# Two gated layers behind a block-sparse attention: token tiles of 512 columns in place of 384, x and the sums in one buffer each

## The chip, the cores and the metric

One core of a Trainium2 chip runs the kernel. The metric is device time in microseconds, the median of several runs. The engines are named as in the profile: PE (TensorE, matmuls), PEld (its weight loads), DVE (VectorE), ACT (ScalarE), POOL (GpSimd), SP (the engine whose queue issues most DMAs).

## What is computed

1536 tokens (2 batches of 768) pass through three stages in float32. The attention has 8 heads of 64; each query sees its neighbours within 16 positions and, for each block of 32 keys, one key (the block's maximum) with one value (the block's mean). Its outputs, one row of 512 numbers per token, feed two layers:

```python
a = softmax(concat(masked(scale * q @ k.T), scale * q @ k_max.T + log(32)))
x = (a @ concat(v, v_mean)).reshape(1536, 512)          # 8 heads side by side
x = (silu(x @ w_gate) * (x @ w_val)) @ w_out            # 512 -> 1536 -> 512
h = x @ w_in                                            # 512 -> 2048
out = (h * clip(h + 3, 0, 6) / 6) @ w_out2              # 2048 -> 512
```

## The kernel before

The layers' matmuls run on operands split in two parts (high and low, type float32r): `three` (L342) issues three matmuls for one product, high by high, low by high, high by low (L352 to L354). Their sum gathers in one PSUM bank of 128 partitions by up to 512 columns.

Tokens are the columns. They come in four tiles of T = 384 (L24, L25). The first layer's hidden units are done in N1 = 4 groups of G1 = 3 blocks of 128, the second's in N2 = 4 groups of G2 = 4 (L31 to L33). For each group and each tile `hidden1` (L437) makes two products per block (gate and value, 4 x 3 matmuls each), ACT takes the tanh out of the bank into u, DVE multiplies twice, and `split` (L420) makes the two parts of the result in a buffer g or gb: one ACT copy, one DVE or POOL subtraction. `out1` (L464) multiplies them by the output weights (4 x 3 x 3 matmuls) and ACT (first group) or DVE (the others) adds the bank into the sums `acc`. After the last group the sums are split again into x2, the second layer's input (L493 to L502). So a group of the first layer costs 72 + 36 = 108 matmuls per tile. `hidden2` (L505, 48 matmuls per group and tile) and `out2` (L525) do the same for the second layer, but out2 has the tokens on the partitions: blocks of 128 tokens, 512 columns of output weights as moving operand, 36 matmuls per tile. The very last block is done in two halves of 256 columns (L526), each stored by its own DMA.

Buffers before the change: one tile x0 to x3 per token tile of shape [128, 2 parts, 4, 384], used again for x2 (tags `x{t}`); one tile acc0 to acc3 of 1536 columns, used for v before and for the output sums afterwards (tags `acc{t}`); and, while attention has not reached them yet, the room of x3 holds three of the first keys (`early_k`, L567) and that of x2 the first queries (`early_q`, L568).

Weights arrive as raw words; `weights` (L378) turns each [128, 512] block into its two parts with five DVE passes (L389, L395, L399, L407, L299) and two ACT passes (L403, L292) (the last subtraction may go to POOL). Two sets of nine buffers, wa and wb, alternate from group to group.

The order is made by a planner (`Plan`, L101): every task has a rank, the engines it may use with an assumed duration, and the names that it reads and writes; `schedule` (L171) simulates the engines with the ring sizes of L280 (mm and mmb: banks, u: 3, g: 5, gb: 5) and issues each engine's instructions in the order it finds. Ranks are then replaced by latest start times and the plan is made anew, up to six times; the one with the earliest end is used (L247). The loop at L829 goes over (layer, group, tile); the hidden tasks of one tile are ranked together with the out tasks of the tile before (`prev`). The rings gb, wb and mmb exist only from the end of attention on (`swap`, L847). While group 0 of the first layer runs, attention for the next token tile is made beside it: its scores, exponentials and outputs go through the banks `at` and `pv` and end in x (L736 to L746).

Of the kernel before, what the change touches and what calls it, by code (L numbers as in the profile page):

```python
# [25 lines left out]
NB = T // QB  # L26
TR = NB // 2
# [250 lines left out]
def tile_kernel(ctx: ExitStack, tc: tile.TileContext, q, k, v, vu, w_gate, w_val, w_out1, w_in2, w_out2, cst, out):  # L278
    nc = tc.nc
    rings = dict(mm=4, mmb=4, at=3, pv=1, wa=9, wb=9, raw=3, bits=2, u=3, g=5, gb=5,  # L280
# [51 lines left out]
    ident = cs[:, :P]  # L332

# [86 lines left out]
    def split(rank, gn, u):  # L420

        add(rank, {"act": 0.43}, lambda: copy("act", new(gn, [P, 2, T], F32R)[:, 0, :], tiles[u]), r=[u], w=[gn])
        add(rank, {"pool": 1.3, "dve": 0.5},
            lambda e: less(e, tiles[gn][:, 1, :], tiles[u], tiles[gn][:, 0, :].bitcast(F32)), r=[u], w=[gn], port=True)
# [9 lines left out]
    xt, x2t, acc, oacc = {}, {}, {}, {}  # L434


    def hidden1(rank, g, t, f, late):  # L437
        bg, bv, u, gn = bank(late), bank(late), ("u", 0, g, t, f), g_name(0, g, t, f, late)

        def tanh():  # L440
            nc.scalar.activation(new(u, [P, T]), tiles[bg][:, :T], AF.Tanh, scale=0.5)

        def gate():
            nc.vector.scalar_tensor_tensor(tiles[u], tiles[u], 1.0, tiles[bg][:, :T], ALU.add, ALU.mult)

        def val():
            nc.vector.tensor_tensor(tiles[u], tiles[u], tiles[bv][:, :T], ALU.mult)  # L447

        for i, bk in enumerate((bg, bv)):
            rank = three(  # L450
                rank, bk, T,
                lambda c, i=i: parts(w_name(0, g, i, f), c * P, P),
                lambda c: (xt[t][:, 0, c, :], xt[t][:, 1, c, :]),
                KC,
                lambda c, i=i: [w_name(0, g, i, f), ("x", t, c)],
                early=g == 0 and t == 0,
            )
            if i == 0:
                add(rank, {"act": 0.4}, tanh, r=[bg], w=[u])
                add(rank, {"dve": 0.47}, gate, r=[bg], w=[u])  # L460
        add(rank, {"dve": 0.47}, val, r=[bv], w=[u])
        split(rank, gn, u)

    def out1(rank, g, t, d, late):  # L464
        bk = bank(late)
        three(
            rank, bk, T,
            lambda f: parts(w_name(0, g, 2, f), d * P, P),
            lambda f: parts(gn_of[0, g, t, f], 0, T),
            G1,  # L470
            lambda f: [w_name(0, g, 2, f), gn_of[0, g, t, f]],
        )
        rank += 1.5
        room = [("A", t)] if g == 0 else []

        def first():
            if t not in acc:
                a = xpool.tile([P, KC * T], F32, tag=f"acc{t}", name=f"acc{t}")
                acc[t] = a.rearrange("p (c t) -> p c t", c=KC)
            nc.scalar.activation(acc[t][:, d, :], tiles[bk][:, :T], AF.Copy, scale=0.5)  # L480

        def more():
            a = acc[t][:, d, :]
            nc.vector.scalar_tensor_tensor(a, tiles[bk][:, :T], 0.5, a, ALU.mult, ALU.add)

        if g == 0:
            add(rank, {"act": 0.4}, first, r=[bk], w=[("acc", t, d)] + room)
        else:
            add(rank, {"dve": 0.47}, more, r=[bk], w=[("acc", t, d)])
        if g < N1 - 1:  # L490
            return

        def high():  # L493
            if t not in x2t:
                x2t[t] = xpool.tile([P, 2, KC, T], F32R, tag=f"x{t}", name=f"x2_{t}")
            copy("act", x2t[t][:, 0, d, :], acc[t][:, d, :])

        def rest(e):
            less(e, x2t[t][:, 1, d, :], acc[t][:, d, :], x2t[t][:, 0, d, :].bitcast(F32))

        add(rank, {"act": 0.43}, high, r=[("acc", t, d)], w=[("x2", t, d)] + [("x", t, c) for c in range(KC)])
        add(rank, {"pool": 1.3, "dve": 0.47}, rest, r=[("acc", t, d)], w=[("x2", t, d)], port=True)  # L502


    def hidden2(rank, g, t, f, late):  # L505
        bk, u, gn = bank(late), ("u", 1, g, t, f), g_name(1, g, t, f, late)
        rank = three(
            rank, bk, T,
            lambda c: parts(w_name(1, g, 0, f), c * P, P),
            lambda c: (x2t[t][:, 0, c, :], x2t[t][:, 1, c, :]),  # L510
            KC,
            lambda c: [w_name(1, g, 0, f), ("x2", t, c)],
        )

        def relu():
            nc.scalar.activation(new(u, [P, T]), tiles[bk][:, :T], AF.Relu, bias=3.0)

        def clip():
            nc.vector.scalar_tensor_tensor(tiles[u], tiles[u], 6.0, tiles[bk][:, :T], ALU.min, ALU.mult)  # L519

        add(rank, {"act": 0.4}, relu, r=[bk], w=[u])
        add(rank, {"dve": 0.47}, clip, r=[bk], w=[u])
        split(rank, gn, u)

    def out2(rank, g, t, m, late, d0=0, n=DM):  # L525
        if (g, t, m, n) == (N2 - 1, NT - 1, T // P - 1, DM):  # L526
            out2(rank, g, t, m, late, 0, DM // 2)
            out2(rank + 1.4, g, t, m, late, DM // 2, DM // 2)
            return
        bk = bank(late)  # L530
        three(
            rank, bk, n,
            lambda f: parts(gn_of[1, g, t, f], m * P, P),
# [4 lines left out]
        rank += 2.6  # L538

        def first():  # L540
            if t not in oacc:
                a = xpool.tile([P, KC * T], F32, tag=f"acc{t}", name=f"oacc{t}")
                oacc[t] = a.rearrange("p (m d) -> p m d", d=DM)
            nc.scalar.activation(oacc[t][:, m, :], tiles[bk], AF.Copy, scale=1.0 / 6.0)

        def more():
            a = oacc[t][:, m, d0 : d0 + n]
            nc.vector.scalar_tensor_tensor(a, tiles[bk][:, :n], 1.0 / 6.0, a, ALU.mult, ALU.add)

        def store():  # L550
            r0 = t * T + m * P
            nc.sync.dma_start(out=out[r0 : r0 + P, d0 : d0 + n], in_=oacc[t][:, m, d0 : d0 + n])

        if g == 0:
            add(rank, {"act": 0.5}, first, r=[bk], w=[("o", t, m)] + [("acc", t, d) for d in range(KC)])
        else:
            add(rank, {"dve": 0.6}, more, r=[bk], w=[("o", t, m)])
        if g == N2 - 1:
            add(rank, {"dma": 0.73 * n / DM}, store, r=[("o", t, m)])
# [65 lines left out]
    def queries(rank, t, c):  # L625
# [94 lines left out]
    def outputs(rank, t, c):  # L720
# [105 lines left out]
    span_g, span_o1 = 2 * G1 * KC * 0.52, KC * G1 * 0.52  # L826
    span_h, span_o2 = G2 * KC * 0.52, T // P * G2 * 0.69
    seq = [(0, g, t) for g in range(N1) for t in range(NT)] + [(1, g, t) for g in range(N2) for t in range(NT)]
    for layer, g, t in seq + [(2, 0, 0)]:  # L829
        late = swap is not None  # L830
        if layer == 0:
            heads_ = [lambda r, f=f: hidden1(r, g, t, f, late) for f in range(G1)]
            span = span_g + (span_o1 if prev else 0)
        elif layer == 1:
            heads_ = [lambda r, f=f: hidden2(r, g, t, f, late) for f in range(G2)]
            span = span_h + (span_o1 if g == 0 and t == 0 else span_o2)
        else:
            heads_, span = [], span_o2
        if (layer, g) == (0, 0) and t + 1 < NT:
            span += SPAN  # L840
        tails = [lambda r, a=a: a[0](r, *a[1:], late) for a in prev]
        step(rank, span, heads_, tails)
        if (layer, g) == (0, 0):
            if t + 1 < NT:
                attention(rank + NEXT, t + 1, (span - NEXT_END) / NP)
            if t + 2 == NT:
# [45 lines left out]
```

## Time and profile before

| | us |
|---|---|
| runs, median of 3 (lowest to highest) | 641.5 (640.62 to 641.62) |
| profiled execution: span, first to last instruction | 638.7 |
| PE busy | 627.4 (98%) in 4492 matmuls |
| DVE busy | 433.9 (68%) |
| ACT busy | 278.8 (44%) |
| POOL busy | 46.4 (7%) |
| DMA | 54.07 MB |

The profile gives no time of the profiled execution beside its span. Matmuls are pipelined: the duration of one is longer than the distance to the next, so rates are read from the starts.

### The profile page before, as it was taken

The numbers are of one execution on the slowest core, as the hardware profiler recorded it, in microseconds if no ns is written. First come the engines' busy times: TensorE is split into PE (matmuls) and PEld (weight loads), VectorE is DVE, ScalarE is ACT, GpSimd is POOL, SyncE is SP. The second block draws the span as 40 slices with busy tenths as digits, with TensorE's granted clock in tenths as the row PEclk, the third lists the DMA queues.
The fourth block names the chain that finished last, engine by engine and source line by source line (L and its number), as shares of the span: only waits on it lengthen the run. The fifth ranks groups of instructions, "written<-read, shape, count | busy, mean of one in ns | idle before, by whom it ended". The sixth has DMA issues, their size and how long they took to land.

```text
span 638.7 us, 11402 instructions
## 1 busy us (share of the span) xinstructions
PE 627.4 (98%) x4492; PEld 589.8 (92%) x4492; DVE 433.9 (68%) x961; ACT 278.8 (44%) x647; POOL 46.4 (7%) x51
## 2 busy tenths in 40 slices
PE   7899999999999999999999999999999999999997
PEld 6787889999999999999999999999999999999996
DVE  5999954899997974397656995286639744344442
ACT  4896886456444431153323554355324422222220
POOL 1234422000000000000000000000000000000000
PEclk9999999999999999999999999999999999999999
DMA  8887340233331411023100323031301000000112
GB/s 314 267 265 233 86 153 3 100 134 131 131 134 65 139 60 67 0 71 129 67 0 1 103 97 100 1 109 56 100 0 67 0 1 1 0 2 1 49 50 99
DMA packets 18917, 54.07 MB, mean 85 GB/s; under 512 B 2608, under 2 KB 5168, under 8 KB 18864
## 3 DMA queue, kind: packets, MB, share of 16 engines
q1 hardware_dynamic: 18576, 52.74, 24.7%
q8 instruction: 35, 0.57, 0.4%
q10 hardware_dynamic: 288, 0.61, 0.3%
q14 instruction: 18, 0.15, 0.1%
HBM read 50.19 MB, written 3.15 MB: 84 GB/s over the span
## 4 chain that ended last, share of the span: by engine, by line
PE 90%; DVE 5%; DMA 2%; ACT 1%; issue 1%; POOL 0%; SPq 0%; POOLq 0%
PE mm L352 16%; PE mm L353 15%; PE mm L354 15%; PE mmb L352 14%; PE mmb L354 13%; PE mmb L353 13%; PE at_s L657 2%; PE pv L728 1%; DMA raw<-in_moe_w_gate 1%; DVE p L677 1%; PE at_t L714 1%; DMA vn<-in_v 1%; DVE ksum L599 1%; DVE v L612 0%; DVE wa L299 0%
## 5 line engine op out<-in xcount | busy, mean ns | idle before, releaser
L352 PE MATMUL mm<-x,wa 128*128 128x384 f32 x196 | 68.4, 349 | 0.0
L353 PE MATMUL mm<-x,wa 128*128 128x384 f32 x196 | 65.9, 336 | 1.1 <-DVE wa L299 1.0
L354 PE MATMUL mm<-x,wa 128*128 128x384 f32 x196 | 65.7, 335 | 0.0
L403 ACT ACTIVATE raw<-raw 128x512 f32<-128x512 f32 x68 | 46.1, 680 | 26.1 <-DVE bits L395 23.0
L353 PE MATMUL mmb<-x,wb 128*128 128x384 f32 x160 | 53.5, 335 | 0.0
L353 PE MATMUL mm<-x,wb 128*128 128x384 f32 x160 | 53.5, 335 | 0.0
L354 PE MATMUL mmb<-x,wb 128*128 128x384 f32 x160 | 53.5, 334 | 0.0
L354 PE MATMUL mm<-x,wb 128*128 128x384 f32 x160 | 53.5, 334 | 0.0
L352 PE MATMUL mm<-x,wb 128*128 128x384 f32 x160 | 53.5, 334 | 0.0
L352 PE MATMUL mmb<-x,wb 128*128 128x384 f32 x160 | 53.5, 334 | 0.0
L292 ACT ACTIVATE g<-u 128x384 fp32r<-128x384 f32 x61 | 32.0, 524 | 39.0 <-DVE u L519 20.5
L399 DVE SCALAR_TENSOR_TENSOR bits<-raw,bits 128x512 uint32<-128x512 uint32 x68 | 47.7, 702 | 0.1
L407 DVE SCALAR_TENSOR_TENSOR bits<-raw,bits 128x512 f32<-128x512 f32 x68 | 47.2, 696 | 0.6 <-ACT raw L403 0.2
L395 DVE SCALAR_TENSOR_TENSOR bits<-raw,bits 128x512 uint32<-128x512 uint32 x68 | 46.4, 684 | 0.3
L299 DVE TENSOR_TENSOR g<-u,g 128x384 fp32r<-128x384 f32 x57 | 31.9, 560 | 20.2 <-ACT g L292 20.1
L292 ACT ACTIVATE gb<-u 128x384 fp32r<-128x384 f32 x51 | 26.8, 525 | 37.5 <-DVE u L447 18.7
L353 PE MATMUL mmb<-x,wa 128*128 128x384 f32 x124 | 41.5, 335 | 0.0
L354 PE MATMUL mmb<-x,wa 128*128 128x384 f32 x124 | 41.5, 334 | 0.0
L352 PE MATMUL mmb<-x,wa 128*128 128x384 f32 x124 | 41.5, 334 | 0.0
L292 ACT ACTIVATE wb<-bits 128x512 fp32r<-128x512 f32 x32 | 20.2, 632 | 46.8 <-DVE bits L407 18.9
L299 DVE TENSOR_TENSOR gb<-u,gb 128x384 fp32r<-128x384 f32 x51 | 28.3, 556 | 17.2 <-ACT gb L292 17.2
L684 ACT ACTIVATE p<-p,st 128x120 f32<-128x120 f32 x96 | 36.7, 384 | 4.9 <-DVE st L677 4.9
(180 smaller groups left out, 1607.8 us busy)
## 6 DMA issues: line engine op xcount, KB each, us to landing
raw<-in_moe_w_out SPq DMA_DIRECT2D x28, 512.0 KB, 3.5
raw<-in_moe_w_in SPq DMA_DIRECT2D x16, 512.0 KB, 3.5
raw<-in_moe_w_gate SPq DMA_DIRECT2D x12, 512.0 KB, 3.7
raw<-in_moe_w_val SPq DMA_DIRECT2D x12, 512.0 KB, 3.5
vn<-in_v SPq DMA_DIRECT2D x8, 384.0 KB, 6.3
vw<-in_vu SPq DMA_DIRECT2D x16, 192.0 KB, 4.3
out<-oacc SPq DMA_DIRECT2D x11, 256.0 KB, 2.0
kT<-in_k SPq DMA_DIRECT2D x5, 400.0 KB, 7.7
```

What stands on the lines that cost most here:

```text
L292: nc.scalar.activation(dst, src, AF.Copy, scale=scale)
L299: eng[e].tensor_tensor(dst, a, b, ALU.subtract)
L352: nc.tensor.matmul(ps, lhsT=lh, rhs=rh, start=j == 0, stop=False)
L353: nc.tensor.matmul(ps, lhsT=ll, rhs=rh, start=False, stop=False)
L354: nc.tensor.matmul(ps, lhsT=lh, rhs=rl, start=False, stop=j == n_k - 1)
L395: nc.vector.scalar_tensor_tensor(t, high_w(), 0xC0000000, t, ALU.bitwise_and, ALU.bitwise_or)
L399: nc.vector.scalar_tensor_tensor(t, low_w(), 29, t, ALU.logical_shift_right, ALU.bitwise_or)
L403: nc.scalar.activation(mag, mag, AF.Abs)
L407: nc.vector.scalar_tensor_tensor(as_f(), mag, 2.0**-15, as_f(), ALU.is_ge, ALU.mult)
L599: nc.vector.tensor_reduce(ksum[c], kT[b, c][:, HALO : HALO + S].rearrange("q (n i) -> q n i", i=BLOCK), AX.X, ALU.max)
L657: nc.tensor.matmul(tiles["at", "s", *names[h]][a * QB : (a + 1) * QB, j, cols], lhsT=tiles[qt][hs, u * QB : (u + 1) * QB], rhs=rhs, start= ...
L684: nc.scalar.activation(a, a, AF.Exp, bias=s[:, 0, n : n + 1], scale=-1.0, accum_out=s[:, 1, n : n + 1])
```

## The change

The layers but for group 0 of the first take token tiles of 4 blocks of 128 (512 columns, 3 tiles); group 0, which runs beside attention, keeps tiles of 3 blocks (384 columns, 4 tiles). A tile is named by (first block, number of blocks). x and x2 share one buffer xs, and v, the first queries, acc and the output sums share one buffer accs; both are laid out by blocks of 128 tokens, so that a tile of either width is a slice. A tile's x for one part and one chunk of 128 features is 3 or 4 runs of 128 columns, 1024 elements apart. The dependencies that the planner is told are by block. The keys get buffers of their own; the first queries lie in accs behind v. u and g tiles grow to 512 columns, and the g ring shrinks from 5 to 4. The planner's assumed durations and spans follow the tile's width. The instructions of each tile, their engines and the weights' work stay as they were. Core of the diff (hidden2, the split, and the other copies follow the same pattern):

```diff
+TB = T // P
+BLOCKS = B * S // P
+WIDE = 4
...
-    rings = dict(mm=4, mmb=4, at=3, pv=1, wa=9, wb=9, raw=3, bits=2, u=3, g=5, gb=5,
+    rings = dict(mm=4, mmb=4, at=3, pv=1, wa=9, wb=9, raw=3, bits=2, u=3, g=4, gb=5,
...
+    xs = xpool.tile([P, BLOCKS, 2, KC, P], F32R, name="x")
+    accs = xpool.tile([P, BLOCKS, KC, P], F32, name="acc")
+
+    def xpart(lh, b0, nb, c):
+        return xs[:, b0 : b0 + nb, lh, c, :]
...
+    def tiles_of(layer, g):
+        nb = TB if (layer, g) == (0, 0) else WIDE
+        return [(b0, nb) for b0 in range(0, BLOCKS, nb)]
...
     def hidden1(rank, g, t, f, late):
+        (b0, nb), n = t, t[1] * P
...
-                rank, bk, T,
+                rank, bk, n,
                 lambda c, i=i: parts(w_name(0, g, i, f), c * P, P),
-                lambda c: (xt[t][:, 0, c, :], xt[t][:, 1, c, :]),
+                lambda c: (xpart(0, b0, nb, c), xpart(1, b0, nb, c)),
                 KC,
-                lambda c, i=i: [w_name(0, g, i, f), ("x", t, c)],
-                early=g == 0 and t == 0,
+                lambda c, i=i: [w_name(0, g, i, f)] + [("x", b, c) for b in range(b0, b0 + nb)],
+                early=g == 0 and b0 == 0,
...
-    early_k = xpool.tile([P, NP - 1, S + 2 * HALO], F32, tag="x3", name="early_k")
-    early_q = xpool.tile([P, 2, NP, T], F32, tag="x2", name="early_q")
-    kT = {(b, c): ap_.tile([P, S + 2 * HALO], F32, name=f"kT{b}_{c}") if b or c == NP - 1 else early_k[:, c]
-          for b in range(B) for c in range(NP)}
+    kT = {(b, c): ap_.tile([P, S + 2 * HALO], F32, name=f"kT{b}_{c}") for b in range(B) for c in range(NP)}
+
+    def acc_room(r, lo, n):
+        return accs[:, r * TB : (r + 1) * TB].rearrange("p b c t -> p (b c t)")[:, lo : lo + n]
...
-                tiles[n] = early_q[:, t, c]
+                tiles[n] = acc_room(q_room(t, c), S + c % 2 * T, T)
...
-    seq = [(0, g, t) for g in range(N1) for t in range(NT)] + [(1, g, t) for g in range(N2) for t in range(NT)]
+    seq = [(layer, g, t) for layer, groups in ((0, N1), (1, N2)) for g in range(groups) for t in tiles_of(layer, g)]
...
-                next_weights(*nxt, rank + span, 3 * span - W_END)
+                next_weights(*nxt, rank + span, len(tiles_of(layer, g)) * span - span - W_END)
```

## Rows read from the trace of the kernel before

**Rows 1.** The page: busy time of each engine, and PE in 40 slices.
```profile
PE 627.4 (98%) x4492; PEld 589.8 (92%) x4492; DVE 433.9 (68%) x961; ACT 278.8 (44%) x647; POOL 46.4 (7%) x51
...
PE   7899999999999999999999999999999999999997
...
PEclk9999999999999999999999999999999999999999
```

**Rows 2.** Engines by stretch (from:to us, length, busy us with instructions, clock).
```profile
core 0: us, PE busy (x) PEld busy (x) DVE busy (x) ACT busy (x) POOL busy (x), PEclk, DMA share, GB/s
0.00:26.23 26.23, 20.99 (x416) 17.99 (x416) 18.83 (x73) 16.31 (x59) 5.90 (x11) 1.00 0.87 286
26.23:50.00 23.77, 22.30 (x368) 18.62 (x368) 23.07 (x88) 21.45 (x76) 7.98 (x10) 1.00 0.86 278
50.00:70.00 20.00, 18.90 (x230) 16.77 (x230) 19.96 (x52) 13.64 (x42) 8.51 (x8) 1.00 0.61 188
70.00:109.00 39.00, 39.00 (x633) 34.35 (x632) 22.84 (x110) 30.05 (x108) 12.99 (x15) 1.00 0.26 83
109.00:136.35 27.35, 27.35 (x160) 27.35 (x158) 24.43 (x47) 13.45 (x25) 0.00 (x0) 1.00 0.27 97
136.35:360.99 224.64, 224.64 (x1298) 224.64 (x1297) 173.31 (x326) 86.72 (x156) 2.58 (x2) 1.00 0.24 80
360.99:634.93 273.94, 273.94 (x1401) 250.04 (x1401) 150.74 (x270) 97.21 (x184) 8.44 (x6) 1.00 0.13 42
```

**Rows 3.** Timeline of PE: first hidden matmuls of group 1 and of layer 2.
```profile
136.35 0.33 PE L352 MATMUL mmb<-x,wb 128*128 128x384 f32 x1
...
360.99 0.33 PE L352 MATMUL mmb<-x,wa 128*128 128x384 f32 x1
```

**Rows 4.** Timeline of PE: first and thirty-first matmul of a run of 512 columns.
```profile
620.56 0.39 PE L352 MATMUL mmb<-wb,gb 128*128 128x512 f32 x1
...
627.36 0.39 PE L352 MATMUL mmb<-wb,gb 128*128 128x512 f32 x1
```

**Rows 5.** Timeline of PE: the same place in two steps of layer 2, thirteen apart.
```profile
395.29 0.34 PE L352 MATMUL mm<-x,wa 128*128 128x384 f32 x1
...
611.69 0.34 PE L352 MATMUL mmb<-x,wb 128*128 128x384 f32 x1
```

**Rows 6.** Instruction groups by form: count, busy us, mean ns, idle before.
```profile
L395 DVE SCALAR_TENSOR_TENSOR bits<-raw,bits 128x512 uint32<-128x512 uint32 x68 | 46.4, 684 | 0.3
L389 DVE TENSOR_SCALAR bits<-raw 128x512 uint32<-128x512 uint32 x68 | 29.2, 432 | 0.1
L447 DVE TENSOR_TENSOR u<-u,mm 128x384 f32<-128x384 f32 x48 | 26.5, 551 | 13.1 <-PE mm L354 12.9
L299 DVE TENSOR_TENSOR wb<-bits,wb 128x512 fp32r<-128x512 f32 x29 | 19.9, 688 | 4.2 <-ACT wb L292 4.1
L548 DVE SCALAR_TENSOR_TENSOR oacc<-mmb,oacc 128x512 f32<-128x512 f32 x18 | 12.4, 691 | 27.7 <-PE mmb L354 27.6
```

**Rows 7.** Engines in group 1 of the first layer (columns as in rows 2).
```profile
136.35:211.23 74.88, 74.88 (x434) 74.88 (x433) 69.27 (x131) 35.84 (x65) 0.00 (x0) 1.00 0.35 120
```

**Rows 8.** What PE waited for, 26 to 109 us: total, times, longest.
```profile
PE mm L353 <- DVE wa L299: 1.0, 1, 1.0
PE at_v L616 <- DVE v L612: 1.0, 3, 0.4
PE at_t L714 <- POOL p L708: 0.2, 1, 0.2
```

**Rows 9.** Timeline of PE: the first matmul that reads g.
```profile
79.55 0.42 PE L352 MATMUL mm<-g,wa 128*128 128x384 f32 x1
```

**Rows 10.** Timelines of ACT and DVE: two passes on one raw tile.
```profile
158.25 0.67 ACT L403 ACTIVATE raw<-raw 128x512 f32<-128x512 f32 x1
...
158.53 0.69 DVE L399 SCALAR_TENSOR_TENSOR bits<-raw,bits 128x512 uint32<-128x512 uint32 x1
```

**Rows 11.** Timeline of the end: the last matmul and the last DVE passes.
```profile
634.54 1.13 DVE L548 SCALAR_TENSOR_TENSOR oacc<-mmb,oacc 128x512 f32<-128x512 f32 x2 [0.36 <-PE mmb L354]
...
634.93 0.28 PE L354 MATMUL mmb<-wb,g 128*128 128x256 f32 x1
```

More of the change, by code (lines that the diff above doesn't have):

```diff
@@ L418, in weights, with split, of_act, of_dve @@
             lambda e: less(e, tiles[wt][:, 1, :], as_f(), tiles[wt][:, 0, :].bitcast(F32)), r=[bits], w=[wt], port=True)
[L420 to L424, printed above, removed]
+    def split(rank, gn, u, n):
+        add(rank, {"act": n / 1200 + 0.11}, lambda: copy("act", new(gn, [P, 2, WIDE * P], F32R)[:, 0, :n], tiles[u][:, :n]),
+            r=[u], w=[gn])
+        add(rank, {"pool": n / 415 + 0.37, "dve": n / 960 + 0.1},
+            lambda e: less(e, tiles[gn][:, 1, :n], tiles[u][:, :n], tiles[gn][:, 0, :n].bitcast(F32)), r=[u], w=[gn], port=True)
+    def of_act(n):
+        return n / 1200 + 0.08
+    def of_dve(n):
+        return n / 960 + 0.07
     gn_of = {}
@@ L473, in out1 @@
         rank += 1.5
-        room = [("A", t)] if g == 0 else []
+        names = [("acc", b, d) for b in range(b0, b0 + nb)]
+        room = [("A", b0 // TB)] + [("q0", t, c) for t in range(2) for c in range(NP) if q_room(t, c) == b0 // TB] if g == 0 else []
+        a = accs[:, b0 : b0 + nb, d, :]
         def first():
[L477 to L480, printed above, removed]
+            nc.scalar.activation(a, cols(tiles[bk][:, :n], nb), AF.Copy, scale=0.5)
         def more():
-            a = acc[t][:, d, :]
-            nc.vector.scalar_tensor_tensor(a, tiles[bk][:, :T], 0.5, a, ALU.mult, ALU.add)
+            nc.vector.scalar_tensor_tensor(a, cols(tiles[bk][:, :n], nb), 0.5, a, ALU.mult, ALU.add)
         if g == 0:
-            add(rank, {"act": 0.4}, first, r=[bk], w=[("acc", t, d)] + room)
+            add(rank, {"act": of_act(n)}, first, r=[bk], w=names + room)
         else:
-            add(rank, {"dve": 0.47}, more, r=[bk], w=[("acc", t, d)])
+            add(rank, {"dve": of_dve(n)}, more, r=[bk], w=names)
         if g < N1 - 1:
@@ L493, in high @@
         def high():
-            if t not in x2t:
-                x2t[t] = xpool.tile([P, 2, KC, T], F32R, tag=f"x{t}", name=f"x2_{t}")
-            copy("act", x2t[t][:, 0, d, :], acc[t][:, d, :])
+            copy("act", xpart(0, b0, nb, d), a)
         def rest(e):
-            less(e, x2t[t][:, 1, d, :], acc[t][:, d, :], x2t[t][:, 0, d, :].bitcast(F32))
-        add(rank, {"act": 0.43}, high, r=[("acc", t, d)], w=[("x2", t, d)] + [("x", t, c) for c in range(KC)])
-        add(rank, {"pool": 1.3, "dve": 0.47}, rest, r=[("acc", t, d)], w=[("x2", t, d)], port=True)
+            less(e, xpart(1, b0, nb, d), a, xpart(0, b0, nb, d).bitcast(F32))
@@ L509, in hidden2 @@
             lambda c: parts(w_name(1, g, 0, f), c * P, P),
-            lambda c: (x2t[t][:, 0, c, :], x2t[t][:, 1, c, :]),
+            lambda c: (xpart(0, b0, nb, c), xpart(1, b0, nb, c)),
             KC,
-            lambda c: [w_name(1, g, 0, f), ("x2", t, c)],
+            lambda c: [w_name(1, g, 0, f)] + [("x2", b, c) for b in range(b0, b0 + nb)],
         )
         def relu():
-            nc.scalar.activation(new(u, [P, T]), tiles[bk][:, :T], AF.Relu, bias=3.0)
+            nc.scalar.activation(new(u, [P, WIDE * P])[:, :n], tiles[bk][:, :n], AF.Relu, bias=3.0)
@@ L518, in clip @@
         def clip():
[L519 to L523, printed above, removed]
+            a = tiles[u][:, :n]
+            nc.vector.scalar_tensor_tensor(a, a, 6.0, tiles[bk][:, :n], ALU.min, ALU.mult)
+        add(rank, {"act": of_act(n)}, relu, r=[bk], w=[u])
+        add(rank, {"dve": of_dve(n)}, clip, r=[bk], w=[u])
@@ L538, in out2 @@
         rank += 2.6
+        a = accs[:, m].rearrange("p c t -> p (c t)")[:, d0 : d0 + n]
         def first():
[L541 to L544, printed above, removed]
+            nc.scalar.activation(a, tiles[bk], AF.Copy, scale=1.0 / 6.0)
         def more():
-            a = oacc[t][:, m, d0 : d0 + n]
             nc.vector.scalar_tensor_tensor(a, tiles[bk][:, :n], 1.0 / 6.0, a, ALU.mult, ALU.add)
         def store():
-            r0 = t * T + m * P
-            nc.sync.dma_start(out=out[r0 : r0 + P, d0 : d0 + n], in_=oacc[t][:, m, d0 : d0 + n])
+            nc.sync.dma_start(out=out[m * P : (m + 1) * P, d0 : d0 + n], in_=a)
         if g == 0:
-            add(rank, {"act": 0.5}, first, r=[bk], w=[("o", t, m)] + [("acc", t, d) for d in range(KC)])
+            add(rank, {"act": of_act(n)}, first, r=[bk], w=[("o", m)] + [("acc", m, d) for d in range(KC)])
         else:
-            add(rank, {"dve": 0.6}, more, r=[bk], w=[("o", t, m)])
+            add(rank, {"dve": of_dve(n)}, more, r=[bk], w=[("o", m)])
         if g == N2 - 1:
-            add(rank, {"dma": 0.73 * n / DM}, store, r=[("o", t, m)])
+            add(rank, {"dma": 0.73 * n / DM}, store, r=[("o", m)])
     vw = [ap_.tile([NK, NB, P], F32, name=f"vw{c}") for c in range(NP)]
@@ L579, in load_v @@
     def load_v(b, c):
-        room = xpool.tile([P, KC * T], F32, tag=f"acc{v_room(b, c)}", name=f"vn{b}_{c}")
-        vn[b, c] = room[:, :S]
+        vn[b, c] = acc_room(v_room(b, c), 0, S)
         nc.sync.dma_start(out=vn[b, c], in_=v[b, c])
@@ L736, in high @@
         def high():
-            if t not in xt:
-                xt[t] = xpool.tile([P, 2, KC, T], F32R, tag=f"x{t}", name=f"x{t}")
-            copy("act", xt[t][:, 0, c, :], tiles[pv])
+            copy("act", xpart(0, t * TB, TB, c), cols(tiles[pv], TB))
         def rest():
-            less("dve", xt[t][:, 1, c, :], tiles[pv], xt[t][:, 0, c, :].bitcast(F32))
+            less("dve", xpart(1, t * TB, TB, c), cols(tiles[pv], TB), xpart(0, t * TB, TB, c).bitcast(F32))
         add(rank, {"pe": 0.85}, weighted, r=[*pts, ("vs", c), ("vw", c)], w=[pv])
-        add(rank, {"act": 0.4}, high, r=[pv], w=[("x", t, c)])
-        last.append(add(rank, {"dve": 0.47}, rest, r=[pv], w=[("x", t, c)]))
+        x = [("x", b, c) for b in range(t * TB, (t + 1) * TB)]
+        add(rank, {"act": 0.4}, high, r=[pv], w=x)
+        last.append(add(rank, {"dve": 0.47}, rest, r=[pv], w=x))
     last = []
@@ L853, in tile_kernel @@
                 swap = add(-1.0, {"none": 0.0}, change, after=last)
-            if t == NT - 1:
+            if n == NT - 1:
                 next_weights(0, 1, rank + NEXT_W, span - 4.0)
-        elif t == 0 and layer < 2:
+        elif layer < 2 and t[0] == 0:
             nxt = (0, g + 1) if layer == 0 and g + 1 < N1 else (1, 0) if layer == 0 else (1, g + 1)
             if nxt[1] < N2:
-                next_weights(*nxt, rank + span, 3 * span - W_END)
+                next_weights(*nxt, rank + span, len(tiles_of(layer, g)) * span - span - W_END)
         prev = []
         if layer == 0:
-            prev = [(out1, g, t, d) for d in range(KC)]
+            prev = [(span_of(0, t)[1] / KC, out1, g, t, d) for d in range(KC)]
         elif layer == 1:
-            prev = [(out2, g, t, m) for m in range(T // P)]
+            prev = [(span_of(1, t)[1] / t[1], out2, g, t, m) for m in range(t[0], t[0] + t[1])]
         rank += span
```

67 lines of the change are left out of this document (41 added, 26 removed).

## The prediction, made before the changed kernel was run

> **What bounds the kernel now.** I read the page's totals first, then the engines by stretch, then TensorE's instructions in order of time, then the instruction groups and waits of the stretches where TensorE isn't full. TensorE (PE) is busy 98% of 638.7 us at the full clock (2.4 GHz) throughout; VectorE (DVE) 68% [rows 1]. By stretch [rows 2] there are three regimes. Up to 70 us attention leads: PE has gaps (20.99 of 26.23, 22.30 of 23.77, 18.90 of 20.00 us) and DVE is full (19.96 of 20.00 us). From 70 to 109 us PE is full, but half with attention. From 109 us to the last matmul at 634.93 us PE has no idle time at all, 526 us on end. So the end is set by how many matmuls follow each other and by how far apart they start; whatever ACT, DVE, POOL and the queues do there is hidden.
>
> Matmul durations overlap, so I take the distance between starts. From the first hidden matmul of group 1 (136.35 us) to the first of the second layer (360.99 us) there are exactly 3 groups x 4 tiles x 108 = 1296 matmuls of 384 columns [rows 3]: 224.64 / 1296 = 173.33 ns each. 384 columns at 2.4 GHz are 160.00 ns; 13.33 ns come on top. The only wide matmuls are those of out2, 512 columns. Where 30 of them follow each other at the end [rows 4], (627.36 - 620.56) / 30 = 226.67 ns = 213.33 + 13.33. The surplus is the same at both widths: it is a price per instruction. Where both widths alternate, it is higher: thirteen steps of the second layer [rows 5], each of 48 matmuls of 384 and 36 of 512 columns, take (611.69 - 395.29) / 13 = 16.646 us, against 48 x 0.17333 + 36 x 0.22667 = 16.480 us: 0.166 us per step is lost in mixing.
>
> **The change, part by part.** The sum is made on the profiled execution: span 638.7 us. The median of the runs is 641.5 us, 2.8 us more, which lie around the span; I carry them over unchanged.
>
> *Fewer, wider matmuls.* Groups 1 to 3 of the first layer have 1296 matmuls of 384 columns, hidden2 has 4 x 4 x 48 = 768: 2064. With 3 tiles in place of 4 they are 972 + 576 = 1548, of 512 columns. The columns stay equal, 516 instructions go: 516 x 13.33 ns = **-6.88 us** (in full: 2064 x 173.33 = 357.8; 1548 x 226.67 = 350.9). All of it lies on the path, since PE has no gap there.
>
> *No more mixing in the second layer.* hidden2 then is as wide as out2. Fifteen of its 16 steps alternate now (the last is the pure run of rows 4): 15 x 0.166 = **-2.5 us**. New mixing arises once, where group 0's last out1 (384) meets group 1's first hidden matmuls (512): one such step, **+0.17 us**. The tail (out2's last block in two halves, its DVE pass, its store [rows 11]) is untouched: 0.
>
> *The moving operand in pieces.* x is now read as 3 or 4 runs of 128 columns with a jump between them. No matmul before does this. Lower bound 0; upper bound that each new run costs what a new instruction costs, 13.33 ns: 1548 x 3 + 432 x 2 = 5508 jumps, 73.4 us. A gain is excluded, the columns being the same. The nearest row is DVE: on every second element (L395, 684 ns) it takes as long as on adjoining ones (L299 into wb, 688 ns) [rows 6]. I take 0.
>
> *One buffer each for x and for the sums.* Writers and readers of different parts now share a buffer; false waits between them would be new. The trace has this case: at 158.25 us ACT (L403) rewrites the odd words of a raw tile, and DVE (L399) starts at 158.53 on the even words of the same tile, before ACT ends at 158.92 [rows 10]. Parts that interleave are kept apart, so 0. Where that failed for x2, the four ACT and four DVE passes per tile at the layers' border would go one behind the other, 8 x 0.69 = 5.5 us if ACT's are priced like DVE's [rows 6]; between the out1 that feeds them and their first reader stand a hidden2 and an out2 tile, about 16.6 us of PE work [rows 5]. Hidden either way.
>
> *ACT and DVE passes.* On 512 columns a DVE pass takes 691 ns (L548), on 384 551 ns (L447) [rows 6]: per group of layer 1, 39 x 0.691 = 26.9 us in place of 52 x 0.551 = 28.7. DVE's tightest dense stretch, group 1 with 69.27 of 74.88 us [rows 7], becomes about 67.5 of 73.4: still covered, no gain. Chains from bank to g grow by about 0.14 us per DVE pass, and stand behind a whole tile of PE work. Weights have one tile less of lead (two tiles of 24.5 us after the first, not three of 18.7), and DVE needs 0.43 + 4 x 0.69 = 3.2 us for one (L389, then four passes like L395 [rows 6]), 29 us for nine, beside 18 us of its own work in those 49: covered, though by 2 us if it had to fit there; it need not, since weights may be taken over sooner, as buffers come free. If that cover fails, the first hidden matmul of the next group waits.
>
> *The loads of q and k, the g ring.* Early k gets room of its own and early q moves into the sums' buffer, in parts that no v occupies. Each load is issued by the same queue with the same bytes, and the sums are first written after those q are consumed, so nothing on SP's or ACT's queue is moved past anything: 0. The g ring goes from 5 to 4, and until attention ends it is the only one. The first out1 starts at 79.55 us [rows 9], when all six hidden results of two tiles are done: then the fifth and sixth must stay in u (three buffers) until out1 gives a g back, where before only the sixth did. PE has work beside that. Bounds: as the plan of this stretch is made anew, it can gain the gaps of 26 to 70 us, 1.47 + 1.10 = 2.6 us; it can lose one split and its handover per tile, 3 x 1.1 = 3.3 us (two passes like L447, ACT's priced like DVE's). PE's named waits there are small, 1.0 + 1.0 + 0.2 us [rows 8]. I take 0.
>
> Sum: -6.88 - 2.5 + 0.17 = **-9.2 us**: span 629.5, time **632.3 us**.
>
> **The rivals.** A measurement of this kernel can tell about 0.2% (1.3 us) from no change.
>
> (a) *Columns are what counts.* If in rows 5 all of the mixing is laid on the wide matmuls, one takes 226.67 + 166 / 36 = 231.3 ns, which is 4/3 of 173.33: then 1548 x 231.3 = 358.0 against 357.8 us, nothing is gained, and out2 stays as slow: 641.7 us, no change. For it: most wide matmuls of the trace are so slow. Against it: rows 4, which run at 226.67 without a neighbour of another width. The Trainium skill's page "TensorE: Matmul & The Clock Gate" (Back-to-back issue gap) puts a warm matmul at N/2.4 + 2.5 ns: nearly all columns. By it, 516 instructions would save an estimated 1.3 us, about 640.2 us. The trace doesn't agree: it has 13.33 ns.
>
> (b) *The jumps in x cost PE time* (slower). Place: each matmul with x as moving operand. At 9.2 us / 5508 = 1.7 ns per jump the gain is used up; at the upper bound of 13.33 ns it is 632.3 + 73.4 = 705.7 us. For it: no row shows PE reading in runs. Against it: the DVE row above.
>
> (c) *The shorter g ring holds the first group up.* The split waits for out1, u stays full, the next hidden tile finds no u, and PE stands for up to one out1, 36 x 0.1733 = 6.2 us: 638.5 us. For it: DVE is full up to 70 us and the order is planned anew. Against it: results that wait in u don't stop PE until all three are held.
>
> **How the numbers follow.** Forecast 73%; (a) 5%; (b) 7%; (c) 15%. Range: below, the forecast with the gaps of 26 to 70 us gained, 629.7; above, (c) in full, 638.5, which takes in the forecast with its 3.3 us (635.6) and half of a 1.7 ns jump. Left out are (a), most of (b), and somewhat more. Faster by over 0.2%: forecast and (c), less a little for two losses at once, 0.86; within 0.2%: (a) and small jumps, 0.06; slower: (b) and its sums with (c), 0.08.
>
> **What would show it.** Right: in group 1 to 3 starts 226.67 ns apart and one group of layer 1 in 73.4 us; in layer 2, 96 matmuls per step in 21.76 us without the sawtooth; 516 fewer matmuls; dense PE from about 109 us on; attention's last matmul where it was, within 2 us. Wrong: hidden matmuls over 226.67 ns while out2's are at it (jumps); all at 231 ns (columns); PE waiting for ACT or DVE between 50 and 135 us (g ring); PE waiting for wa or wb at a group's start (weights). The forecast falls altogether if starts of x matmuls are not constant at 226.67 ns.

## The result, and the profile after

The changed kernel takes 632.15 us (median of 4 runs, 632.13 to 632.21) against 641.54 us for the kernel before (4 runs, 640.62 to 641.62): ratio 0.9856, 95% interval 0.9843 to 0.987. The profiled execution took 632.16 us at a span of 630.4 us; the span before was 638.7 us.

The page of the changed kernel, answering to [rows 1]: busy time of each engine, and PE and its granted clock in 40 slices.

```profile
span 630.4 us, 10224 instructions
...
PE 618.9 (98%) x3976; PEld 523.1 (83%) x3976; DVE 426.7 (68%) x881; ACT 269.2 (43%) x594; POOL 51.5 (8%) x55
...
PE   8899999999999999999999999999999999999997
...
PEclk9999999999999999999999999999999999999999
```

There are 4492 - 3976 = 516 matmuls fewer. PE's idle time is as it was (638.7 - 627.4 = 11.3 us before, 630.4 - 618.9 = 11.5 us after): the kernel is shorter because its matmuls take less time, not because a gap was closed.

Engines by stretch in the changed kernel, cut at the same events as [rows 2]; the last line is group 1 of the first layer, as [rows 7].

```profile
core 0: us, PE busy (x) PEld busy (x) DVE busy (x) ACT busy (x) POOL busy (x), PEclk, DMA share, GB/s
0.00:26.78 26.78, 21.98 (x419) 19.27 (x420) 18.71 (x72) 16.61 (x60) 5.90 (x11) 1.00 0.88 293
26.78:50.00 23.22, 21.16 (x360) 17.77 (x357) 22.52 (x88) 21.18 (x76) 7.28 (x9) 1.00 0.82 267
50.00:70.00 20.00, 18.90 (x226) 16.52 (x227) 19.96 (x52) 12.98 (x39) 9.18 (x9) 1.00 0.63 191
70.00:109.00 39.00, 38.99 (x633) 34.36 (x633) 23.33 (x110) 30.26 (x110) 12.74 (x15) 1.00 0.26 83
109.00:137.09 28.09, 28.09 (x162) 28.09 (x163) 23.55 (x45) 13.82 (x25) 0.00 (x0) 1.00 0.27 94
137.09:358.59 221.50, 221.50 (x989) 184.66 (x989) 172.76 (x289) 84.89 (x139) 12.29 (x10) 1.00 0.24 84
358.59:626.60 268.01, 268.01 (x1195) 222.32 (x1193) 145.11 (x229) 89.44 (x148) 4.12 (x3) 1.00 0.12 41
137.09:210.50 73.41, 73.41 (x335) 62.06 (x335) 70.02 (x121) 36.92 (x61) 6.48 (x5) 1.00 0.37 129
```

The stretches up to 109 us look as they did. From 109 us to the last matmul PE has no idle time, as before. The three groups of the first layer went from 224.64 to 221.50 us, the second layer from 273.94 to 268.01. Together, first hidden matmul of group 1 to last matmul: 634.93 - 136.35 = 498.58 us before, 626.60 - 137.09 = 489.51 us after, **9.07 us less**. Group 1 itself starts 137.09 - 136.35 = **0.74 us later**. After the last matmul come 3.8 us in both. 9.07 - 0.74 = 8.3 us, the difference of the spans.

Timeline of PE in the changed kernel: the same place in two steps of the first layer that lie six steps apart, in two steps of the second layer that lie nine apart, and the last matmul.

```profile
137.09 0.39 PE L368 MATMUL mmb<-x,wb 128*128 128x512 f32 x1
...
187.23 0.39 PE L368 MATMUL mmb<-x,wb 128*128 128x512 f32 x1
...
334.11 0.39 PE L368 MATMUL mmb<-x,wb 128*128 128x512 f32 x1
...
400.07 0.39 PE L368 MATMUL mmb<-x,wa 128*128 128x512 f32 x1
...
595.91 0.39 PE L368 MATMUL mmb<-x,wb 128*128 128x512 f32 x1
...
626.60 0.28 PE L370 MATMUL mmb<-wb,gb_(8, 4)_3_5667 128*128 128x256 f32 x1
```

First layer: (334.11 - 187.23) / (6 x 108) = 226.67 ns per matmul. Second layer: (595.91 - 400.07) / 9 = 21.76 us per step of 96 matmuls, again 226.67 ns, where a step of 84 matmuls of two widths took 16.646 us [rows 5]. That is the rate of the pure run of [rows 4], now with x in four runs of 128 columns as the moving operand.

What PE waited for from 26.78 to 137 us (total us, times, longest), answering to [rows 8]:

```profile
PE mm L369 <- DVE wa L302: 1.4, 2, 1.0
PE at_v L640 <- DVE v L636: 1.0, 3, 0.4
PE pv L752 <- DVE x L302: 0.3, 1, 0.3
PE at_t L738 <- POOL p L732: 0.2, 1, 0.2
```

The three waits of before and a short one of pv, some 0.7 us more in all. None names u, g or acc. From 109 to 626 us the view has no wait of PE.

### The profile page after: what moved, and what is told of

Its sections match the earlier page's. It is cut to its first block, busy times and chain, and to the rows that moved or that the text cites. A ratio compares the mean times of both kernels' runs of the same rounds, so it can differ in the third digit from the quotient of the medians.

```text
span 630.4 us, 10224 instructions
## 1 busy us (share of the span) xinstructions
PE 618.9 (98%) x3976; PEld 523.1 (83%) x3976; DVE 426.7 (68%) x881; ACT 269.2 (43%) x594; POOL 51.5 (8%) x55
## 4 chain that ended last, share of the span: by engine, by line
PE 91%; DVE 5%; DMA 3%; issue 0%; ACT 0%
PE mm L368 16%; PE mm L369 15%; PE mm L370 15%; PE mmb L368 13%; PE mmb L369 13%; PE mmb L370 13%; PE at_s L681 2%; DMA kT<-in_k 1%; DMA raw<-in_moe_w_val 1%; PE pv L752 1%; PE at_t L738 1%; DVE p L701 1%; DVE bits L415 1%; DVE wa L302 0%; DVE ksum L623 0%
## 5 line engine op out<-in xcount | busy, mean ns | idle before, releaser
L368 PE MATMUL mm<-x,wa 128*128 128x384 f32 (+1 forms) x168 | 63.5, 378 | 0.0
L369 PE MATMUL mm<-x,wa 128*128 128x384 f32 (+1 forms) x168 | 61.0, 363 | 1.4 <-DVE wa L302 1.4
L370 PE MATMUL mm<-x,wa 128*128 128x384 f32 (+1 forms) x168 | 60.9, 362 | 0.0
L415 DVE SCALAR_TENSOR_TENSOR bits<-raw,bits 128x512 uint32<-128x512 uint32 x68 | 48.8, 722 | 0.1
L369 PE MATMUL mmb<-x,wb 128*128 128x512 f32 x120 | 46.7, 389 | 0.0
L370 PE MATMUL mmb<-x,wb 128*128 128x512 f32 x120 | 46.7, 389 | 0.0
L368 PE MATMUL mmb<-x,wb 128*128 128x512 f32 x120 | 46.7, 389 | 0.0
L368 PE MATMUL mm<-x,wb 128*128 128x512 f32 x120 | 46.7, 389 | 0.0
L369 PE MATMUL mm<-x,wb 128*128 128x512 f32 x120 | 46.7, 389 | 0.0
L370 PE MATMUL mm<-x,wb 128*128 128x512 f32 x120 | 46.7, 389 | 0.0
L368 PE MATMUL mmb<-x,wa 128*128 128x512 f32 (+1 forms) x96 | 36.7, 382 | 0.0
L369 PE MATMUL mmb<-x,wa 128*128 128x512 f32 (+1 forms) x96 | 36.7, 382 | 0.0
L370 PE MATMUL mmb<-x,wa 128*128 128x512 f32 (+1 forms) x96 | 36.7, 382 | 0.0
L369 PEld LDWEIGHTS mm<-x,wa 128*128 128x128 f32 x168 | 31.6, 188 | 5.2 <-DVE wa L302 1.9
L571 DVE SCALAR_TENSOR_TENSOR acc<-mmb,acc 128x512 f32<-128x512 f32 (+1 forms) x19 | 12.9, 676 | 33.7 <-PE mmb L370 33.6
L295 ACT ACTIVATE wa<-bits 128x512 fp32r<-128x512 f32 x33 | 20.8, 631 | 34.4 <-DVE bits L423 13.7
L368 PEld LDWEIGHTS mm<-x,wa 128*128 128x128 f32 x168 | 31.5, 188 | 4.7
```

The source lines that it names most:

```text
L295: nc.scalar.activation(dst, src, AF.Copy, scale=scale)
L368: nc.tensor.matmul(ps, lhsT=lh, rhs=rh, start=j == 0, stop=False)
L369: nc.tensor.matmul(ps, lhsT=ll, rhs=rh, start=False, stop=False)
L370: nc.tensor.matmul(ps, lhsT=lh, rhs=rl, start=False, stop=j == n_k - 1)
L415: nc.vector.scalar_tensor_tensor(t, low_w(), 29, t, ALU.logical_shift_right, ALU.bitwise_or)
```

## The experiments

The theory: a matmul of the layers, with the weight load that each of them has, costs its columns at 2.4 GHz plus 13.33 ns, and a step that mixes 384 and 512 columns costs 0.166 us more; where x lies, how it is cut, and the g ring cost nothing. The rivals: the new layout has a price or a gain of its own, hidden in the sum; the gain is in one layer alone; or the 0.74 us at the start is what the shorter g ring costs.

Since the profiled executions differ in when group 1 starts, the table sets the two parts side by side. The "dense part" goes from the first hidden matmul of group 1 to the last matmul, both read from the timeline of PE. The last column is a time of dummies, matmuls on a tile of zeros whose result nobody reads: the kernel opens with them, and fills gaps of its plan with them. It is the time that six of them in a row take after 7 us, and is explained below.

| kernel (profiled execution) | group 1 starts | last matmul | dense part | against before | six dummies |
|---|---|---|---|---|---|
| before | 136.35 | 634.93 | 498.58 | | 0.51 |
| layout_only | 136.30 | 634.88 | 498.58 | 0.00 | 0.51 |
| layout_g4 | 137.27 | 635.86 | 498.59 | +0.01 | 0.81 |
| wide_l1 | 137.28 | 631.95 | 494.67 | -3.91 | 0.82 |
| wide_l2 | 137.24 | 631.08 | 493.84 | -4.74 | 0.82 |
| the change | 137.09 | 626.60 | 489.51 | -9.07 | 0.82 |
| wide_g3 | 136.62 | 626.12 | 489.50 | -9.08 | 0.51 |
| wide_g5gb4 | 136.47 | 625.98 | 489.51 | -9.07 | 0.51 |
| after_again | 136.67 | 626.17 | 489.50 | -9.08 | 0.51 |
| cols256 | 137.66 | 649.13 | 511.47 | +12.89 | 0.82 |
| before_idle54 | 136.39 | 634.98 | 498.59 | +0.01 | none |
| wide_idle54 | 136.72 | 626.23 | 489.51 | -9.07 | none |
| wide_idle54_b | 136.61 | 626.12 | 489.51 | -9.07 | none |

**The layout alone.** Everything of the change but the width: tiles of 3 blocks everywhere, u and g tiles of 384 columns, once with the g ring at 5 and once at 4.

```diff
-WIDE = 4
+WIDE = 3
...
-        nb = TB if (layer, g) == (0, 0) else WIDE
+        nb = TB
...
-    rings = dict(..., g=4, gb=5,
+    rings = dict(..., g=5, gb=5,
```

The last pair of lines is in layout_only alone.

> The block layout, the shared buffers and the new places of the early keys and queries, but tiles of 384 everywhere and a g ring of 5. Forecast: 641.5 us, no change; starts of hidden matmuls 173.33 ns apart although x is read in three runs; the end of attention at 108.0 us as in the kernel before. If a jump costs PE 1.7 ns: 2496 - 576 matmuls that read x, two jumps each, +6.5 us or so. If it is the layout that moved the end of attention to 108.75 us in the changed kernel: 642.2 us.

> As layout_only, with the g ring of 4. If the ring is what delays the end of attention by 0.74 us in the changed kernel: 642.2 us with attention ending at 108.7 us, and layout_only at 108.0. If the ring is free, as forecast: both alike.

Measured: 641.25 us (12 runs) against 641.26 (23 runs of the kernel before on the same chip), ratio 1.0002, 0.9993 to 1.0011; with the ring of 4, 641.44 us (11 runs), ratio 1.0003, 0.9994 to 1.0012. Timeline of PE in layout_only, first hidden matmuls of group 1 and of layer 2:

```profile
136.30 0.33 PE L368 MATMUL mmb<-x,wb 128*128 128x384 f32 x1
...
360.94 0.33 PE L368 MATMUL mmb<-x,wa 128*128 128x384 f32 x1
```

360.94 - 136.30 = 224.64 us, to the hundredth what it was [rows 3], and each x matmul is now read in three runs. So the jumps, the shared buffers and the interleaved writers cost nothing and bring nothing; neither does the ring of 4 at the old width. In the profiles the sign that was set down for a costly ring did come up, group 1 at 136.30 us with the ring of 5 and at 137.27 with the ring of 4, but the medians don't follow it, and the late start turns out below to have another source.

**One layer at a time.** Wide tiles in the first layer alone, then in the second alone:

```diff
-        nb = TB if (layer, g) == (0, 0) else WIDE
+        nb = TB if layer == 1 or g == 0 else WIDE
```

```diff
-        nb = TB if (layer, g) == (0, 0) else WIDE
+        nb = TB if layer == 0 else WIDE
```

> The changed kernel, but only groups 1 to 3 of the first layer take tiles of 512 columns; the second layer keeps 384. A price of 13.33 ns per matmul: 324 matmuls fewer are -4.3 us; the second layer alternates between 384 and 512 as before; two borders between widths (group 0 to 1, layer 1 to 2) +0.17 us each: 637.5 us, and starts in groups 1 to 3 are 226.67 ns apart. If columns are what counts: 641.5 us or more. If weights or DVE came late with the wider tiles, PE would show gaps at the starts of groups 1 to 3.

> The other half: only the second layer takes 512 columns, all of the first keeps 384. A price per matmul and a price of mixing: 192 matmuls fewer are -2.6 us, and the mixing of fifteen steps goes, -2.5 us, one border +0.17 us: 636.6 us. If the mixing were no loss of its own (wide matmuls just slower): 641.5 us less at most 2.6 us, 638.9 us.

Measured: wide_l1 637.53 us (5 runs), ratio 0.9944, 0.9932 to 0.9956; wide_l2 636.65 us (5 runs), ratio 0.9924, 0.9913 to 0.9936. Timeline of PE in wide_l1: six steps of the first layer, then the sawtooth of the second:

```profile
187.42 0.39 PE L368 MATMUL mmb<-x,wb 128*128 128x512 f32 x1
...
334.30 0.39 PE L368 MATMUL mmb<-x,wb 128*128 128x512 f32 x1
...
392.31 0.34 PE L368 MATMUL mm<-x,wa 128*128 128x384 f32 x1
...
608.71 0.34 PE L368 MATMUL mmb<-x,wb 128*128 128x384 f32 x1
```

(608.71 - 392.31) / 13 = 16.646 us: the second layer, left at two widths, is exactly as slow as before [rows 5]. Timeline of PE in wide_l2: eleven steps of the first layer, nine of the second:

```profile
139.84 0.33 PE L368 MATMUL mmb<-x,wb 128*128 128x384 f32 x1
...
345.76 0.33 PE L368 MATMUL mmb<-x,wb 128*128 128x384 f32 x1
...
404.55 0.39 PE L368 MATMUL mmb<-x,wa 128*128 128x512 f32 x1
...
600.39 0.39 PE L368 MATMUL mmb<-x,wb 128*128 128x512 f32 x1
```

(345.76 - 139.84) / 11 = 18.72 us and (600.39 - 404.55) / 9 = 21.76 us. In the dense part the first layer gives 3.91 us: 324 matmuls fewer x 13.33 = 4.32, less two borders between widths (groups 0 and 1, and the layers'), 0.2 us each. The second gives 4.74 us: 192 x 13.33 = 2.56 plus the mixing, less one such border. So more than half of the gain comes from the layer with the fewer matmuls, and about half of that from the mixing. The parts' sum, 8.65, falls 0.42 short of 9.07 because the border between the layers is in both variants and not in the full change.

**The other direction.** Tiles of 256 columns, to see whether the price per instruction holds at a third width:

```diff
-        nb = TB if (layer, g) == (0, 0) else WIDE
+        nb = TB if (layer, g) == (0, 0) else 2
```

> The change the other way: tiles of 256 columns (two blocks) in all groups but the first, so 3096 matmuls of 256 columns in place of the 2064 of 384. A price of 13.33 ns per matmul: starts 120.0 ns apart, 3096 x 120.0 - 357.8 = +13.8 us; alternating 256 and 512 in the second layer costs between nothing and what 384 and 512 cost (2.5 us, which then stays), so 652.8 to 655.3 us. If columns are what counts: 641.5 us. If weight loads or DVE bound at this width: above 655.3 us, with PE gaps or starts over 120 ns.

Measured: 654.62 us (4 runs, 654.47 to 655.9) against 641.55 (11 runs), ratio 1.0211, 1.0198 to 1.0224. Timeline of PE in cols256: thirteen steps of the first layer, twenty of the second:

```profile
193.75 0.28 PE L368 MATMUL mmb<-x,wb 128*128 128x256 f32 x1
...
362.23 0.28 PE L368 MATMUL mmb<-x,wb 128*128 128x256 f32 x1
...
397.26 0.28 PE L368 MATMUL mm<-x,wa 128*128 128x256 f32 x1
...
622.60 0.28 PE L368 MATMUL mm<-x,wb 128*128 128x256 f32 x1
```

(362.23 - 193.75) / (13 x 108) = 120.00 ns = 106.67 + 13.33: the third point on the same line. A step of the second layer (48 matmuls of 256 and 24 of 512 columns) takes (622.60 - 397.26) / 20 = 11.267 us against 48 x 0.120 + 24 x 0.22667 = 11.200, so here mixing costs only 0.067 us per step. So the mixing price differs from pair to pair of widths. The sum agrees with the dense part: 1032 instructions more x 13.33 = 13.76 us, mixing 24 x 0.067 - 2.43 = -0.8, together +12.9 against +12.89.

**The g ring.** The changed kernel with a ring of 3, and with one of 5 (gb then has 4, since two rings of 5 such tiles have no room):

```diff
-    rings = dict(..., g=4, gb=5,
+    rings = dict(..., g=3, gb=5,
```

```diff
-    rings = dict(..., g=4, gb=5,
+    rings = dict(..., g=5, gb=4,
```

> The changed kernel with a g ring of 3 in place of 4. If the ring is what holds up the first group (rival c), one buffer fewer makes it worse: attention ends after 108.75 us, PE has gaps before 136 us, 633 us or more; in layer 2 only seven buffers for the eight results of two tiles may show gaps too. If the ring is free: 632.2 us.

> The changed kernel with the buffer given to the other ring: g of 5, gb of 4 (both at 5 do not fit). While attention runs only g counts, so group 0 has the ring of the kernel before. If the ring costs the 0.74 us: attention ends at 108.0 us and the time is 631.4 us. If not: 632.2 us.

Measured: 632.05 us (4 runs) and 631.92 us (6 runs), ratios 0.9855 (0.9841 to 0.9869) and 0.9865 (0.9843 to 0.9886). Even a ring of 3 holds nothing up: its group 1 starts at 136.62 us, earlier than with 4 in the profile of the change. Nor is the 0.74 us a price of the ring: in wide_g5gb4 and in the change PE works off the same matmuls in the same order, and yet by 11 us one is late and the other is not.

**Where the 0.74 us come from.** The table sorts itself. In the executions whose six dummies take 0.51 us, group 1 starts at 136.30 to 136.67 us; where they take 0.81 or 0.82 us, at 137.09 to 137.66 us. The change itself is found with either: 0.82 in its first profile, 0.51 in after_again, which is the changed kernel once more. Timeline of PE at the start, first the kernel before, then the change:

```profile
7.88 0.51 PE L789 MATMUL mm_none<-zeros 128*128 128x128 bf16 x6
```

```profile
8.46 0.82 PE L812 MATMUL mm_none<-zeros 128*128 128x128 bf16 x6
```

PE runs slowly there for a few us. Engines by stretch in layout_g4, early in the execution (columns as above):

```profile
6.00:8.00 2.00, 1.16 (x50) 1.05 (x51) 1.32 (x2) 0.00 (x0) 0.00 (x0) 0.97 1.04 393
8.00:10.00 2.00, 2.00 (x20) 1.85 (x19) 2.00 (x11) 1.10 (x4) 0.00 (x0) 0.50 1.05 391
10.00:12.00 2.00, 2.00 (x59) 1.80 (x56) 1.35 (x7) 1.97 (x11) 0.00 (x0) 0.67 1.03 245
```

From 8 to 10 us the granted clock is 0.50, the 1.2 GHz level, in 20 matmuls at full occupancy. Attention's first scores come late, and DVE, which has no gap from its first pass on v (at 7.52 us) up to there, waits for them. Timeline of DVE in the change:

```profile
12.05 0.28 DVE L701 CUSTOM_DVE_ANT_0 p<-at_s,cs 128x120 f32<-128x120 f32 x1 [0.64 <-PE at_s L681]
```

That first pass on v waits for a DMA, and with it the rest of the start can be accounted for. Timelines of DVE in the kernel before, the change and after_again:

```profile
7.48 0.95 DVE L612 TENSOR_REDUCE v<-vn 128x24 f32<-128x768 f32 x1 [0.66 <-DMA vn<-in_v]
```

```profile
7.52 0.95 DVE L636 TENSOR_REDUCE v<-acc 128x24 f32<-128x768 f32 x1 [0.93 <-DMA acc<-in_v]
```

```profile
7.79 0.95 DVE L636 TENSOR_REDUCE v<-acc 128x24 f32<-128x768 f32 x1 [1.15 <-DMA acc<-in_v]
```

In all eight profiled executions without slow dummies group 1 starts 128.86 to 128.92 us after this pass, with rings of 3, 4 and 5 alike; in the five with slow dummies, 129.57 to 129.81 us after it. So of the 0.74 us of the change 0.70 are PE's slow start (129.57 against 128.87) and 0.04 the landing of v; after_again is 0.32 us later than the kernel before, and 0.31 of that is the landing. What moves it was not tried.

The granted clock's record in the traces shows two kinds of slow start. In the change, wide_l1 and wide_l2 the record begins only at 10.05, 10.32 and 10.13 us, with the full level, and up to there the dummies start 107 ns apart, as they do at the 1.2 GHz level in layout_g4, and 56 ns afterwards. In layout_g4 and cols256 the clock is at its full level from 4.5 us on, falls to the 1.2 GHz level at 7.9 and is back at 11.3. (Where the record has no entry yet, the views print 1.00.) In the other eight it begins at 3.94 to 6.79 us, also after dummies 107 ns apart, and the full level stays to the last matmul.

Ahead of that stretch PE idles for about 1 us in the change, between its opening dummies (the last ends at 5.65 us) and the first scores. So the next experiment was to fill that gap in both kernels, with 54 opening dummies in place of 40, and to repeat the change itself. (The plan adds 2 to the 40; with 54 it drops them, and 7 of the fillers that follow.)

```diff
-IDLE = 40
+IDLE = 54
```

> The changed kernel once more, beside the next one. In its first profile PE's matmuls between 6.6 and 9 us started at half pace (six dummy matmuls took 0.82 us, in the kernel before 0.51), and attention ended 0.74 us later than before. If that belongs to the execution and not to the program, this profile may show either pace; the median stays at 632.2 us within 0.5 us. If it belongs to the change: again half pace, attention's end at 108.7 us.

> The changed kernel with 54 dummy matmuls at the start in place of 40, so that PE's idle second between 5.6 and 6.6 us is filled. If the pace between 6.6 and 12 us hangs on that gap: full pace in the profile, attention's end at 108.0 us, and a median up to 0.7 us lower, 631.5 us. If not: 632.2 us. If the extra dummies run past the first scores: up to 0.3 us higher.

> The kernel before, with 54 dummy matmuls at the start in place of 40. If the start's pace hangs on PE's gap before the first scores, and not on this change: the runs of the kernel before spread from 640.5 to 642, these stay within 0.4 us of each other, near 640.6 us. If not: the same spread as the kernel before.

> The changed kernel with 54 dummies once more: 631.6 us within 0.3 us in all runs, 9.0 us less than before_idle54, which is the change without the start's scatter. If the first result was chance: 632.2 us with a spread of 1 us.

Timelines of PE in wide_idle54, before_idle54 and wide_idle54_b, their first work:

```profile
0.99 5.94 PE L812 MATMUL mm_none<-zeros 128*128 128x128 bf16 x54 [0.99 <-POOL zeros L805]
7.04 0.31 PE L681 MATMUL at_s<-ksum,acc 64*64 64x24 f32 x8
```

```profile
0.99 4.93 PE L789 MATMUL mm_none<-zeros 128*128 128x128 bf16 x54 [0.99 <-POOL zeros L782]
6.84 0.31 PE L657 MATMUL at_s<-ksum,early_q 64*64 64x24 f32 x8 [0.92 <-DVE ksum L599]
```

```profile
0.99 4.58 PE L812 MATMUL mm_none<-zeros 128*128 128x128 bf16 x54 [0.99 <-POOL zeros L805]
6.68 0.31 PE L681 MATMUL at_s<-ksum,acc 64*64 64x24 f32 x8 [1.11 <-DVE ksum L623]
```

Measured: after_again 632.25 us (4 runs, 631.75 to 633.29; ratio 0.987, 0.9853 to 0.9886); wide_idle54 631.63 us (4 runs, 631.52 to 631.82; ratio 0.9855, 0.984 to 0.9869); before_idle54 640.77 us (11 runs, 640.63 to 641.41) beside 641.58 us (15 runs, 640.78 to 643.25), ratio 0.9988, 0.9979 to 0.9997; wide_idle54_b 631.69 us (5 runs, 631.31 to 632.14; ratio 0.9846, 0.9833 to 0.9859). All three profiled executions with 54 dummies are on time, but only wide_idle54 has the gap filled: in the two others the clock rose while the dummies ran (at 4.68 and 3.94 us), these end at 5.92 and 5.57 us, and PE idles 0.92 and 1.11 us, as long as in the slow start of the change (0.99 us). So the runs show that 54 dummies help, and not that the filled gap is why. The mean granted clock of every execution bears the first out: none of the 20 with 54 dummies is under 0.999, and 44 of the 111 with 40 are at 0.997 or less. (This counts the second kind of start alone: where the record begins late, as in the change, the mean reads 1.00.) The kernel before gains 0.8 us by it, the change some 0.6 us (after_again against wide_idle54). The runs are closer together, though not within the 0.3 and 0.4 us that were expected. On the same chip, both with 54 dummies, the difference is 640.77 - 631.69 = 9.08 us, as in the dense parts (9.07). The change with 54 dummies is the fastest version found, but it stands only some 0.1% below the change as it is, and the intervals overlap.

## Why the prediction was right

Forecast were 632.3 us and a sum of -9.2 us; measured were 632.15 us and, in the dense part, -9.07 us. Step by step:

- *Fewer, wider matmuls, -6.88 us.* As forecast: 516 instructions fewer and starts exactly 226.67 ns apart in both layers. The price per instruction was read from two widths; a third (120.00 ns at 256 columns) confirmed it. Since each matmul here has a weight load of its own, no run shows which of the two bears the price. The Trainium skill's page "TensorE: Matmul & The Clock Gate" (Back-to-back issue gap) gives N/2.4 + 2.5 ns as the gap of a single warm matmul; an estimate by it would be 109.2, 162.5 and 215.8 ns at the three widths. These traces do not agree: they show 120.00, 173.33 and 226.67.
- *No more mixing, -2.5 us.* Measured 2.4 us: the starts of the dense part lie 2.43 us over what their widths alone would give before (at 120.00, 173.33 and 226.67 ns), and 0.23 us after, of which 0.17 are the new border. wide_l1 kept it, wide_l2 lost it. This settles rival (a): out2's matmuls were never slow by themselves. The step with the least certain reason, a loss that belongs to neither width, held.
- *One new border, +0.17 us.* Measured 0.17 us at group 1's start.
- *Jumps in x, 0.* Exact spacing in every wide step, and the layout alone at 1.0002: rival (b) has no part in it. Its bound was too high: the 5508 jumps count out1's matmuls, whose moving operand is g, in one run. Of the 1548 wide matmuls 648 + 576 read x, and 288 of the 432 of group 0: 4248 jumps, at 13.33 ns 56.6 us in place of 73.4.
- *Shared buffers, ACT and DVE passes, weights, 0.* No wait of PE after 109 us. One size here was off: DVE in group 1 was to be busy 67.5 of 73.4 us and is 70.02. It has 10 instructions fewer there (131, now 121) where 13 were forecast, and its 18 passes of L415 took 759 ns each, before (L399) 684. The engines did not all stay as they were: the plan gave POOL five of the weights' subtractions in this group, and none before. The cover is thinner than forecast, 3.4 us in place of 5.9.
- *The g ring, 0, and rival (c).* Rings of 3, 4 and 5 give the same dense part, and starts of group 1 within 0.2 us (136.62, 136.67, 136.47), or 0.02 us when counted from the first pass on v. Of the bounds of -2.6 to +3.3 us nothing was used; the gaps of 26 to 70 us stayed.
- *The 2.8 us around the span.* This term was mis-sized, by an error of pairing. The span of 638.7 us belongs to executions of about 640.7 us, 1.9 to 2.1 us more (layout_only's profile has 638.7 and 640.79); the median of 641.5 us belongs to executions that lose some 0.8 us at the start. The profiled execution of the change was one of the latter, at 630.4 and 632.16 us. So the 2.8 us carried over held about 0.8 us of late start; since the change's median holds some of that too, the error did not show in the time. That the time came out within 0.15 us of the forecast is in part luck; that the dense part came out within 0.13 us of it is not.

## What to carry to other kernels

Where TensorE has no gap, as here from 109 us on, count its instructions, not only its columns. Read the distance between starts at two widths: the part that doesn't grow with the width is saved with every instruction removed, and steps that alternate widths can cost more than the sum of both rates. Before adding a span and a median, check that the profiled execution and the median run begin alike: half a us at the start is more than several of the terms argued over.

## What the runs showed that was not expected

- PE does not start at the full clock, as the prediction had it ("throughout"). In the kernel before the record begins at 5.63 us, and the opening dummies up to there start 107 ns apart, later ones 56 ns. When the full level comes, and whether it holds, differs between executions of one and the same program: 10.05 us in the change, 5.83 in after_again.
- Idling of PE before the first scores does not sort the executions: 0.99 to 2.08 us in the five slow starts, 0.1 to 1.5 in the eight others. The two in which the clock fell again have the two longest, 1.68 (layout_g4) and 2.08 us (cols256); two are too few to make a rule of it. What decides is open.
- A granted clock of 1.00 in a view may mean that the record has no entry there: in the change it reads 1.00 in every slice, while six dummies take 0.82 us in place of 0.51.
- Mixing 384 with 512 columns cost 0.166 us per step, mixing 256 with 512 only 0.067 us. Why the pair matters was not tried.
- PEld, busy throughout groups 1 to 3 before (224.64 us of 224.64 [rows 2]), now has 184.66 of 221.50 us. Its being full was no sign of a limit: matmuls of 256 columns, with more weight loads for the same columns, followed each other at the same 13.33 ns over their columns, and there too PEld is busy throughout (168.48 of 168.48 us in the thirteen steps).
